# Step 5's clearing, the first batch's order, and the last batch with GEMM1's beginning

## The chip, the cores and the metric

One core of a Trainium2 chip runs the whole kernel. The metric is the device time of one execution in microseconds (us), as the median over runs.

## The reference

```python
def rmsnorm(x, g): return x / sqrt(mean(x*x, -1) + 1e-6) * g
q, k, v: (8 batches, 12 heads, 448 tokens, 64)          # float32
scores = (1/sqrt(64)) * rmsnorm(q, g_q) @ rmsnorm(k, g_k).T
attn   = exp(scores - max) / (sum + 1e-9)
x      = (attn @ v) as (3584 tokens, 768)
expert = token_ids * 2654435761 % 8                      # each token has one of 8 experts
out[mask_e] = relu(x[mask_e] @ w1[e]) @ w2[e]            # w1 (8, 768, 1024), w2 (8, 1024, 768)
```

## The kernel before

**Attention.** The work is cut into 48 steps: step s is a pair of heads of batch s // 6. For a step, `score` (L630) makes four blocks of scores in PSUM: j = 0, 1, 2 are two heads by 128 keys by 448 queries (two matmuls), j = 3 is the last 64 keys of both heads. `expo` (L647) turns each block into probabilities on ScalarE: 896 columns for j < 3, 448 for j = 3. `av_part` (L657) multiplies them with v in three parts; `row_sums` and `put_x` (L690, L697) divide by the row sums on VectorE and, after the sixth step of a batch, store the batch to `x_scratch` in HBM.

Ahead of that, q and k of a group of steps are squared (`sqq`, `sqk`, L361), summed by matmuls with an identity (`sumq`, `sumk`, L381), reduced (`redq`, `redk`), put through ln and exp on ScalarE (`ln`, `er`), multiplied in (`nq`, `nk`, L417), turned by TensorE (`Tq`, `Tk`, L588) and copied out of PSUM as `qT` and `kT` (L608; kT is scaled by a column `g_col` there). Step 0 alone is group 0, steps 1 and 2 are group 1, steps 3 to 5 are group 2. Step 5 is loaded by itself: `zero:3` (L743) clears the padding of its two raw tiles by two ScalarE copies (L756, L757), issues its six transfers on SP's queue (`load_one`, L732) and then the transfer of the token ids. All other q, k and v loads go through POOL's queue, in the order of L768 to L785.

**Who sets the order.** Each engine runs its instructions in program order, and program order is written out by hand: `emit` (L852) reads a text of tokens, `kind:step.part`, and issues each token's instructions. `@A` puts a square or a copy on ScalarE in place of VectorE, `@S` takes a PSUM tile from the ring of score tiles (3 tiles of two banks) in place of the one bank `qkT_ps`. One text covers batches 0 and 1, the text `steady` is used for each of batches 2 to 7. `spin:n` issues n dummy matmuls of 448 columns that fill TensorE's time at the start.

**The seam.** Tokens are grouped by expert. Three tiles of 128 tokens of expert 0, all from batches 0 to 6, are gathered from `x_scratch` by POOL (L230) while batch 7 runs. After the last token of `steady`, `early_xT` (L642) turns them one after the other: six transposes into a PSUM tile of the score ring (L242) and one copy into `xT_e` (L243; VectorE for tiles 0 and 1, ScalarE for tile 2). Then the last step's `av_part`, `row_sums` and `put_x` follow, and then the GEMMs.

**GEMMs.** For each expert GEMM1 (`gemm1`, L951) makes eight blocks of hidden units, each of six matmuls over 384 token columns (expert 0) or 480, with a ReLU copy each; GEMM2 (`gemm2`, L966) follows, and POOL scatters the rows of the result. Weights of later experts are loaded meanwhile. For expert 0 the routing table of the other experts is made on VectorE between the blocks.

The order around the seam, from `steady` with batch 7 as its batch: `... sc:5.0 kT:6 exp:4.1 exp:4.3 sc:5.1 rec:3 exp:5.0 sc:5.2 Tq:6 x:3 v:3 av:4.0 av:4.1 qT:6 sc:5.3 sumq:2.1 exp:5.1 exp:5.2 sqk:2.0 sc:6.0 nk:8 exp:5.3 av:4.2 ...` (tokens of steps beyond 47 issue nothing).

Of the kernel before, what the change touches and what calls it, by code (L numbers as in the profile page):

```python
# [20 lines left out]
def kernel(  # L21
# [242 lines left out]
    with tc.manual_schedule(), \  # L264
# [587 lines left out]
        def emit(text, b):  # L852
# [24 lines left out]
            sumq:2.0 redk:2.0 av:0.0 redq:2.0 sc:1.2 av:0.1 v:1 sc:1.3 ln:2 er:2 av:0.2  # L877
            sc:1.1 nq:3 rec:0 exp:1.2 exp:1.3 Tq@S:3 exp:1.1 nk:3 sc:2.0 Tk:3 x:0 exp:2.0
            sc:2.1 exp:2.1 qT:3 kT:3 sc:2.2 av:1.0 exp:2.2 sc:2.3 av:1.1 av:1.2 sqk:3.0
            sc:4.0 exp:2.3 nk:5 sumk:3.0 rec:1 exp:4.0 sc:3.0 x:1 sc:3.1 av:2.0 redk:3.0  # L880
            av:2.1 sqk:4.0 exp:3.0 nq:5 sumk:4.0 v:2 sc:3.2 av:2.2 redk:4.0 sqq:3.0 rec:2
            exp:3.1 Tk@S:5 sc:3.3 kT:5 x:2 sumq:3.0 exp:3.2 sc:4.3 sc:4.2 exp:3.3 redq:3.0
            exp:4.3 ln:3 er:3 sc:4.1 exp:4.2 av:3.0 sqk:4.1 Tq:5 exp:4.1 sqq:4.0 av:3.1 qT:5
            sumk@S:4.1 nq:6 av:3.2 nk:6 redk:4.1 sc:5.0 rec:3 sumq:4.0 sc:5.3 sc:5.1 exp:5.0
            exp:5.3 redq:4.0 sqq:4.1 x:3 Tk:6 exp:5.1 Tq@S:6 kT:6 sumq@S:4.1 redq:4.1 qT@A:6
            av:4.0 av:4.1 ln:4 sc:5.2 av:4.2 er:4 exp:5.2 sc:6.0 sqk:5.0 v:4 sc:7.0 sumk:5.0
            exp:6.0 rec:4 sc:6.3 x:4 av:5.0 av:5.1 exp:7.0 exp:6.3 nq:8 sc:7.3 redk:5.0 nk:8
            exp:7.3 v:3 Tq:8 sc:6.1 av:5.2 qT:8 sc:6.2 Tk@S:8 rec:5 sqq:5.0 exp:6.1 sc:7.1
            sumq:5.0 x:5 exp:6.2 av:6.0 sc:7.2 exp:7.1 exp:7.2 kT:8 sc:8.0 sqq:5.1 redq:5.0
            sc:8.1 nq:10 exp:8.0 av:6.1 sumq:5.1 nk:10 redq:5.1 exp:8.1 av:6.2 sc:8.3 rec:6  # L890
            Tk:10 x:6 sc:9.0 sc:8.2 exp:8.3 av:7.0 sc:9.3 exp:9.0 kT:10 Tq:10 av:7.1 av:7.2
            sc:9.1 sqk:5.1 qT:10 exp:8.2 rec:7 sc:9.2 x:7 v:5 exp:9.3 exp:9.1 sumk:5.1
            redk:5.1 exp:9.2 sqq:6.0 av:8.0 av:8.1 av:8.2 sc:10.0 sc:10.2 sc:10.1 rec:8 ln:5
            er:5 x:8 nk:12 exp:10.0 sumq:6.0 av:9.0 exp:10.1 sc:10.3 redq:6.0 Tk:12 av:9.1
            nq:12 av:9.2 kT:12 rec:9 exp:10.2 sc:11.0 exp:10.3 exp:11.0 sc:11.2 exp:11.2
            sc:11.3 x:9 Tq:12 sqq:6.1 av:10.0 av:10.1 sc:11.1 qT:12 nk:14 av:10.2 exp:11.3
            sc:12.0 sumq:6.1 sc:12.2 rec:10 exp:11.1 sc:12.1 x:10 exp:12.0 exp:12.2 redq:6.1
            Tk:14 sc:12.3 sqk:6.0 exp:12.1
# [25 lines left out]
    with tc.manual_schedule(), \  # L924
# [26 lines left out]
        def gemm1(w1v, xT, h_sb, c0, c1, both=True, after=()):  # L951
            for fo in range(FO):
                h_ps = ps_h.tile([P, 512], FP32, name="h_ps")
                for co in range(CO):
                    nc.tensor.matmul(h_ps[:, :c1 - c0], lhsT=w1v[:, co, fo, :],  # L955
                                     rhs=xT[:, co, c0:c1],
                                     start=(co == 0), stop=(co == CO - 1))
# [320 lines left out]
```

## Time and profile before

| | |
|---|---|
| Median of 3 runs | 338.56 us (337.82 to 338.94) |
| The profiled execution | 337.33 us |
| Its span | 335.8 us |
| TensorE (PE) busy | 322.8 us, 96% |
| VectorE (DVE) busy | 197.7 us, 59% |
| ScalarE (ACT) busy | 188.2 us, 56% |
| GpSimd (POOL) busy | 147.0 us, 44% |

Times of rows are microseconds from the span's start. A timeline row has the start, the length, engine, line, operation, the tiles written and read with their shapes, how many instructions are merged in it (x), and in brackets the idle time before it with what ended it. Lengths of neighbours overlap, since an instruction's end includes its write; what an engine needs for one in a dense row is the distance of starts. A row of windows has, for each stretch, its length, each engine's busy time with its count of instructions, the granted TensorE clock (1.00 is 2.4 GHz), the DMA engines' share and GB/s. A row of DMA issues has the tiles, the issuing queue, count, KB each, and us from issue to landing.

### The profile page before, as it was taken

To read this page: it belongs to the slowest core of one execution; us is meant where nothing else is said; L and a number is where in the kernel's file an instruction comes from. 1 tells how busy PE (TensorE), PEld (TensorE's weight loads), DVE (VectorE), ACT (ScalarE), POOL (GpSimd) and SP (SyncE) were. 2 spreads that over 40 slices of the span, in tenths; PEclk is the share of its full clock that TensorE was granted. 3 is DMA by queue.
4 is the path that set the end of the run, shared out by engine and by line. 5 is a ranking of instruction groups with operands and counts; after the bars stand their busy time and mean duration, and the time that the engine had idled before them with its cause. 6 is when DMAs were issued, how large, how long until landed. Compare 5 with 4: busy or idle time off the path is not lost. (4 is left out here: it accounts for less than half of the span.)

```text
span 335.8 us, 9161 instructions
## 1 busy us (share of the span) xinstructions
PE 322.8 (96%) x3873; PEld 224.9 (67%) x3873; DVE 197.7 (59%) x427; ACT 188.2 (56%) x287; POOL 147.0 (44%) x207
## 2 busy tenths in 40 slices
PE   6899999999999999998999999999999999999992
PEld 3567776777777776666677667677676676766761
DVE  4699999998989899984792342232332323222210
ACT  3799999999999999998442211212022020221211
POOL 8799925423440100003655844538556374203122
PEclk9999999999999999999999999999999999999997
DMA  6999999999999999432587899999999999923012
GB/s 118 205 202 204 214 228 197 242 200 237 203 243 210 248 227 236 84 84 72 156 169 224 162 209 247 264 280 247 255 262 263 268 254 265 267 34 133 25 64 105
DMA packets 45602, 65.54 MB, mean 195 GB/s; under 512 B 12727, under 2 KB 33423, under 8 KB 45432
## 3 DMA queue, kind: packets, MB, share of 16 engines
q0 software_dynamic: 39072, 58.32, 86.0%
q1 hardware_dynamic: 6328, 6.50, 7.2%
q8 instruction: 31, 0.51, 0.6%
q10 hardware_dynamic: 160, 0.11, 0.1%
q14 instruction: 11, 0.09, 0.1%
HBM read 89.29 MB, written 17.30 MB: 317 GB/s over the span
## 5 line engine op out<-in xcount | busy, mean ns | idle before, releaser
L652 ACT ACTIVATE expT<-sc_ps 128x896 bf16<-128x896 f32 x144 | 125.0, 960 | 0.9 <-PE sc_ps L636 0.6
L972 PEld LDWEIGHTS <-h_sb 128*128 128x128 f16 (+1 forms) x512 | 51.3, 104 | 30.2
L972 PE MATMUL o_ps<-w_sb,h_sb 128*128 128x512 f16 (+3 forms) x384 | 66.2, 326 | 0.0
L985 POOL DMA_INDIRECT out_dram<-o_sb,gidx x32 | 33.8, 1055 | 63.4 <-ACT o_sb L982 30.9
L959 ACT ACTIVATE h_sb<-h_ps 128x480 f16<-128x480 f32 (+1 forms) x36 | 19.9, 553 | 67.3 <-PE h_ps L955 67.3
L230 POOL DMA_INDIRECT kr<-x_scratch,gidx x32 | 32.7, 1022 | 50.8 <-DVE oc L578 36.7
L955 PEld LDWEIGHTS <-w_sb 128*128 128x128 f16 x288 | 38.9, 136 | 16.2
L955 PE MATMUL h_ps<-xT,w_sb 128*128 128x480 f16 x240 | 49.4, 366 | 0.0
L982 ACT COPY o_sb<-o_ps 128x768 f32<-128x768 f32 x16 | 12.8, 799 | 60.4 <-PE o_ps L972 55.2
L961 DVE TENSOR_SCALAR h_sb<-h_ps 128x480 f16<-128x480 f32 x28 | 18.4, 658 | 47.2 <-PE h_ps L955 47.2
L636 PE MATMUL sc_ps<-qT,kT 64*128 64x448 f16 x288 | 44.4, 356 | 0.7 <-DVE qT L628 0.4
L671 PEld LDWEIGHTS <-expT 128*128 128x128 bf16 x864 | 37.8, 97 | 9.0 <-DVE x_sb L702 4.1
L671 PE MATMUL av_ps<-v,expT 128*128 128x65 bf16 x846 | 42.3, 193 | 0.1
L982 DVE COPY o_sb<-o_ps 128x768 f32<-128x768 f32 (+1 forms) x15 | 14.3, 956 | 37.1 <-PE o_ps L972 30.3
L305 POOL DMA_DIRECT2D vr<-in_v_dram x36 | 23.7, 669 | 20.1 <-DMA kr<-in_k_dram 10.8
L702 DVE TENSOR_TENSOR x_sb<-av_ps,srec 128x448 f16<-128x448 f32 x47 | 29.2, 622 | 1.3
L655 ACT ACTIVATE expT<-sc_ps 128x448 bf16<-128x448 f32 x48 | 28.6, 599 | 0.1
L386 PEld LDWEIGHTS <-ident 128*128 128x128 f16 x576 | 22.6, 97 | 8.2 <-issue 3.6
L676 PE MATMUL av_ps<-v,expT 128*128 128x130 bf16 x141 | 24.5, 220 | 0.0
L972 PE MATMUL o_ps<-kr,h_sb 128*128 128x512 f16 (+3 forms) x128 | 21.6, 326 | 0.0
L243 DVE COPY xT<-xT_ps 128x768 f16<-128x768 f16 (+1 forms) x21 | 11.0, 524 | 17.9 <-PE xT_ps L242 17.7
L955 PE MATMUL h_ps<-xT,qr 128*128 128x480 f16 x96 | 19.8, 366 | 0.0
(218 smaller groups left out, 437.9 us busy)
## 6 DMA issues: line engine op xcount, KB each, us to landing
w_sb<-in_moe_w_dram POOLq DMA_DIRECT2D x18, 512.0 KB, 12.4
w_sb<-in_moe_w_dram POOLq DMA_DIRECT2D x8, 768.0 KB, 13.1
kr<-in_k_dram POOLq DMA_DIRECT2D x7, 672.0 KB, 14.9
qr<-in_q_dram POOLq DMA_DIRECT2D x7, 672.0 KB, 12.4
x_scratch<-x_sb SPq DMA_DIRECT2D x15, 288.0 KB, 6.8
...
```

Source lines behind the costliest of these rows:

```text
L230: nc.gpsimd.indirect_dma_start(out=xg[0:idx.shape[0], :], out_offset=None, in_=x_dram[0:rows, :], in_offset=bass.IndirectOffsetOnAxis(ap=i ...
L305: eng.dma_start(out=dst[64 * half:64 * half + 64, :, s0:s0 + cnt, :].rearrange("p n s d -> p n (s d)"), in_=runs(t, h0 + HP * hh, 1, n, to ...
L636: nc.tensor.matmul(sc[:, hh, :S], lhsT=kT[64 * hh:64 * hh + 64, P * j:P * j + P], rhs=qT[64 * hh:64 * hh + 64, :], start=True, stop=True)
L652: nc.scalar.activation(expT[:, 2 * j:2 * j + 2, :], sc[:, :, :S], AF.Exp, bias=0.0, scale=1.0)
L655: nc.scalar.activation(expT[:, 6, :], sc[:, 0, :S], AF.Exp, bias=0.0, scale=1.0)
L671: nc.tensor.matmul(av[:, 2 * t + hh, :], lhsT=expT[:, tl(hh, j), P * t:P * t + P], rhs=v8[:, i, vs(hh, j), 0:D + 1], start=(hh == 0 and t ...
L676: nc.tensor.matmul(av[:, 2 * t:2 * t + 2, :], lhsT=expT[:, 6, P * t:P * t + P], rhs=v8[:, i, 0::7, 0:D + 1], start=False, stop=False)
L702: nc.vector.tensor_tensor(out=xs[b][:, :, hp * D:hp * D + D], in0=av[:, :, :D], in1=srec[:, :, None].to_broadcast([P, SL, D]), op=ALU.mult)
L955: nc.tensor.matmul(h_ps[:, :c1 - c0], lhsT=w1v[:, co, fo, :], rhs=xT[:, co, c0:c1], start=(co == 0), stop=(co == CO - 1))
L972: nc.tensor.matmul(o_ps[d0 > 0][0:w, d0:d1], lhsT=h_sb[:, fo, col * P:col * P + w], rhs=w2_sb[:, fo, d0:d1], start=(fo == 0), stop=(fo == ...
L982: (nc.vector.tensor_copy if col % 2 else nc.scalar.copy)(o_sb[0:w], o_ps[0][0:w])
L985: scat = nc.gpsimd.indirect_dma_start(out=out[:, :], out_offset=bass.IndirectOffsetOnAxis(ap=idx[0:w], axis=0), in_=o_sb[0:w], in_offset=N ...
```

## The change

1. `zero:3` clears step 5's padding by two VectorE memsets, and stands later in the order, so that step 5's six transfers and the token ids are issued later.
2. Batches 0 and 1 get a new order. In its beginning both squares of step 0 and both of its copies out of PSUM are on ScalarE; of later copies, those of kT for steps 3, 5 and 6 are on ScalarE, and qT of step 6 and `sqq:2.0.1` (step 5's q) come to VectorE.
3. Batch 7 gets an order of its own, `tail`, in which expert 0's turns (`turn`) and the last step's products (`last`) stand among the others. The last step's products run over j first, so that only those with j = 2 need the third block of probabilities and only part 1 the fourth.
4. `xT_e` is laid out by token tile first; GEMM1 of expert 0 makes the first 256 columns of its first two blocks before their last 128 (`apart=2`).

```diff
-    xT_e = m_xe.tile([P, CO, CAP], FP16, name="xT_e")
+    xT_e = m_xe.tile([P, CAP // P, CO, P], FP16, name="xT_e")
@@ put_xT
-        (copy or nc.vector.tensor_copy)(xT[:, :, col * P:col * P + n], xT_ps[:, :, 0:n])
+        dst = xT[:, col] if xT is xT_e else xT[:, :, col * P:(col + 1) * P]
+        (copy or nc.vector.tensor_copy)(dst[:, :, 0:n], xT_ps[:, :, 0:n])
@@ early_xT and av_part take their PSUM tile by flag: S score ring, Q qkT_ps, else av_ps
+        def bank_of(flag):
...
+        def av_last(part):
...
+            if part == 0:
+                bank = bank_of(flag)
...
+                for j in range(3):
+                    for hh in range(2):
+                        for t in range(3):
+                            nc.tensor.matmul(pend[s][1][:, 2 * t + hh, :],
+                                             lhsT=expT[:, tl(hh, j), P * t:P * t + P],
...
+                return
+            for t in range(3):
+                nc.tensor.matmul(av[:, 2 * t:2 * t + 2, :], lhsT=expT[:, 6, P * t:P * t + P],
...
+            for j in range(4):
+                for hh in range(2):
+                    nc.tensor.matmul(av[64 * hh:64 * hh + 64, 6, :],
...
@@ zero
-                z = warm[:, 0:4 * D].rearrange("p (s d) -> p s d", d=D)
-                nc.scalar.copy(raw(1, HP - 1)[:, 0::7], z[:, 0:2])
-                nc.scalar.copy(raw(0, HP - 1)[64:P, 3::4], z[64:P, 0:2])
+                V.memset(raw(1, HP - 1)[:, 0::7], 0.0)
+                V.memset(raw(0, HP - 1)[64:P, 3::4], 0.0)
                 load_one(HP - 1)
                 setup1()
@@ the order of batches 0 and 1, its first lines
-            zero:0 zero:1 zero:2 zero:6 zero:7 spin:11 sqk:0.0 zero:3 sqq@A:0.0 sumk@S:0.0
-            redk:0.0 sumq@S:0.0 ln:0.1.2 redq:0.0 er:0.1.2 ln:0.0.1 er:0.0.1 sqk@A:1.0
-            gain:0 spin:2 nk:0 spin:4 gain:1 Tk@S:0 nq:0 sumk@S:1.0 gain:2 sqq:1.0 Tq@S:0
-            redk:1.0 sumq:1.0 kT:0 redq:1.0 qT@A:0 sc:0.0 ln:1 er:1 sc:0.1 spin:5 exp:0.0
-            nk:1 Tk@S:1 sc:0.3 nq:1 Tq:1 sqk:2.0.0 kT:1 qT:1 exp:0.1 sqq:2.0.0 v:0
-            sqk@A:2.0.1 sc:0.2 exp:0.3 sumk@S:2.0 sc:1.0 sqq@A:2.0.1 exp:0.2 exp:1.0
...
+            zero:0 zero:1 zero:2 zero:6 zero:7 spin:11 sqq@A:0.0 sumq@S:0.0 redq:0.0
+            sqk@A:0.0 ln:0.0.1 gain:0 er:0.0.1 sumk@S:0.0 gain:1 redk:0.0 ln:0.1.2 spin:8
+            er:0.1.2 zero:3 gain:2 nk:0 sqk@A:1.0 Tk:0 nq:0 Tq@S:0 kT@A:0 sumk@S:1.0 sqq:1.0
+            qT@A:0 redk:1.0 sumq@S:1.0 sc:0.0 redq:1.0 ln:1 sc:0.1 sc:0.2 er:1 nq:1 exp:0.0
+            nk:1 v:0 spin:3 spin:1 Tq:1 qT:1 exp:0.1 Tk@S:1 kT:1 sqk:2.0.0 sc:0.3 exp:0.2
+            exp:0.3 av:0.0 sc:1.0 sqq:2.0.0 sqk@A:2.0.1 sc:1.1 exp:1.0 sc:1.2 sumk:2.0
+            exp:1.1 sqq:2.0.1 av:0.1 sumq@S:2.0 redk:2.0 exp:1.2 av:0.2 v:1 redq:2.0 sc:2.0
+            v:2 rec:0 ln:2 er:2 nk:3 sc:2.2 x:0 sc:1.3 Tk:3 exp:2.0 nq:3 nq:5 exp:1.3 sc:2.3
+            av:1.0 exp:2.2 sqk:3.0 av:1.1 Tq@S:3 qT:3 sc:2.1 exp:2.3 kT@A:3 Tq@S:5 exp:2.1
...
@@ batch 7
+        tail = """
+            av:-1.0 av:-1.1 sc:1.0 kT:2 av:-1.2 exp:0.3 exp:1.0 nq:2 sc:1.1 nq:4 rec:-1
...
+            rec:2 x:2 sc:4.1 sc:4.3 av:3.0 av:3.1 av:3.2 rec:3 sc:5.0 exp:4.1 exp:4.3 sc:5.1
+            av@Q:4.0 x:3 av:4.1 exp:5.0 turn@S:0 sc:5.2 exp:5.1 av:4.2 rec:4 x:4 sc:5.3
+            exp:5.2 exp:5.3 turn@S:1 last:0 turn@Q:2 last:1 rec:5 x:5
+        """
         for b in range(2, B):
-            emit(steady, b)
-        for kt in range(KT - 1):
-            early_xT(kt)
-        for part in range(3):
-            av_part(NS - 1, part)
-        row_sums(NS - 1)
-        put_x(NS - 1)
+            emit(steady if b < B - 1 else tail, b)
@@ gemm1(..., apart=0), called with apart=2 for expert 0
+            for fo in range(apart):
+                products(fo, c0, c1 - P)
             for fo in range(FO):
...
+                products(fo, c1 - P if fo < apart else c0, c1)
+                h_ps = banks.pop(fo)
```

## Rows read from the trace of the kernel before

**Rows 1.** Busy time of each engine by stage, from the view of windows.

```profile
40.00:140.00 100.00, 99.17 (x1833) 72.14 (x1830) 94.16 (x208) 99.58 (x148) 26.10 (x37) 1.00 1.20 220
140.00:160.00 20.00, 18.57 (x324) 12.77 (x325) 13.58 (x35) 18.62 (x27) 3.15 (x3) 1.00 0.25 66
160.00:318.00 158.00, 158.00 (x1058) 108.62 (x1057) 56.16 (x101) 34.60 (x57) 79.13 (x87) 1.00 0.87 212
```

**Rows 2.** Timeline of TensorE at the seam.

```profile
157.44 0.93 PE L242 MATMUL sc_ps<-ident,kr 128*128 128x128 f16 x12 [0.32 <-ACT expT L652]
158.21 0.53 PE L671 MATMUL av_ps<-v,expT 128*128 128x65 bf16 x12
...
159.03 0.32 PE L685 MATMUL av_ps<-v,expT 128*64 128x65 bf16 x8
159.28 2.12 PE L955 MATMUL h_ps<-xT_e,w_sb 128*128 128x384 f16 x12
```

**Rows 3.** Timeline of ScalarE at the seam.

```profile
154.67 2.71 ACT L652 ACTIVATE expT<-sc_ps 128x896 bf16<-128x896 f32 x3
157.08 0.74 ACT L655 ACTIVATE expT<-sc_ps 128x448 bf16<-128x448 f32 x1
158.41 0.80 ACT L243 COPY xT_e<-sc_ps 128x768 f16<-128x768 f16 x1 [0.58 <-PE sc_ps L242]
```

**Rows 4.** Timeline of POOL: the third gather of expert 0's tokens.

```profile
153.99 1.00 POOL L230 DMA_INDIRECT kr<-x_scratch,gidx  x1 [0.30 <-issue]
```

**Rows 5.** DMA issues in the stretch of that gather: its time to landing.

```profile
kr<-x_scratch,gidx POOLq DMA_INDIRECT x1, 3.1
```

**Rows 6.** Timeline of VectorE at the seam: step 46's output, the first two turns.

```profile
156.92 0.62 DVE L702 TENSOR_TENSOR x_sb<-qkT_ps,srec 128x448 f16<-128x448 f32 x1
157.46 1.06 DVE L243 COPY xT_e<-sc_ps 128x768 f16<-128x768 f16 x2
```

**Rows 7.** Timeline of ScalarE over batches 0 and 1.

```profile
5.72 0.63 ACT L372 ACTIVATE sq_q<-expT 128x512 f16<-128x512 f32 x1 [2.60 <-DMA expT<-in_q_dram]
...
10.18 0.54 ACT L622 ACTIVATE qT<-sc_ps 128x448 f16<-128x448 f16 x1 [0.88 <-PE sc_ps L601]
...
11.90 1.71 ACT L652 ACTIVATE expT<-sc_ps 128x896 bf16<-128x896 f32 x2
...
16.25 0.92 ACT L652 ACTIVATE expT<-sc_ps 128x896 bf16<-128x896 f32 x1 [0.36 <-PE sc_ps L636]
...
22.66 3.40 ACT L652 ACTIVATE expT<-sc_ps 128x896 bf16<-128x896 f32 x4
...
31.13 0.94 ACT L622 ACTIVATE qT<-sc_ps 128x896 f16<-128x896 f16 x1
```

**Rows 8.** Timeline of VectorE at the start: a memset, step 0's norms, group 1's squares.

```profile
1.59 0.11 DVE L741 MEMSET expT<- 64x64 f32 x1
...
7.63 1.28 DVE L434 TENSOR_TENSOR n_one<-expT,rr 128x512 f16<-128x512 f32 x2
...
9.95 0.63 DVE L374 TENSOR_TENSOR sq_q<-qr 128x896 f16<-128x896 f16 x1 [0.97 <-DMA qr<-in_q_dram]
```

**Rows 9.** Timeline of TensorE at the start: six spins, the first scores.

```profile
7.12 1.29 PE L791 MATMUL av_ps<-hi 128*128 128x448 f16 x6
...
11.15 0.55 PE L636 MATMUL sc_ps<-qT,kT 64*128 64x448 f16 x4
```

**Rows 10.** Timeline of SP: step 5's first four issues and its last.

```profile
3.59 2.42 SPq L305 DMA_DIRECT2D kr<-in_k_dram  x4
...
6.76 0.61 SPq L299 DMA_DIRECT2D qr<-in_q_dram  x1
```

**Rows 11.** DMA issues: step 5's k and q from SP; v issued at 8.86 by POOL.

```profile
kr<-in_k_dram SPq DMA_DIRECT2D x1, 64.0 KB, 4.0
...
qr<-in_q_dram SPq DMA_DIRECT2D x1, 96.0 KB, 5.9
...
vr<-in_v_dram POOLq DMA_DIRECT2D x1, 96.0 KB, 7.8
```

More of the change, by code (lines that the diff above doesn't have):

```diff
@@ L640, in score @@
                                  start=True, stop=True)
+        def bank_of(flag):
+            if flag == "S":
+                return ps_sc.tile([P, 2, 512], FP32, name="sc_ps")[:, 0]
+            if flag == "Q":
+                return ps_qk.tile([P, 512], FP32, name="qkT_ps")
+            return ps_av.tile([P, 512], FP32, name="av_ps")
         def early_xT(kt):
-            bank = ps_sc.tile([P, 2, 512], FP32, name="sc_ps")[:, 0]
+            bank = bank_of(flag)[:]
             put_xT(xg_e[:, kt], xT_e, kt, bank.bitcast(FP16)[:, 0:DIN],
@@ L661, in av_part @@
             if part == 0:
-                bank = (ps_qk.tile([P, 512], FP32, name="qkT_ps") if s == NS - 2 else
-                        ps_av.tile([P, 512], FP32, name="av_ps"))
+                bank = bank_of(flag)
                 pend[s] += [bank[:, 0:SP].rearrange("p (a d) -> p a d", a=SL), bank]
@@ L688, in av_part @@
                                          start=False, stop=(j == 3))
+        def av_last(part):
+            s = NS - 1
+            c = chunk_of[s]
+            i, v8 = s - chunks[c], v8_tiles[c % NV8]
+            vs = lambda hh, j: (0, 7)[hh] if j == 3 else 1 + 3 * hh + j
+            tl = lambda hh, j: 6 if j == 3 else 2 * j + hh
+            expT = pend[s][0]
+            if part == 0:
+                bank = bank_of(flag)
+                pend[s] += [bank[:, 0:SP].rearrange("p (a d) -> p a d", a=SL), bank]
+                for j in range(3):
[3 more added lines that the diff above has]
+                                             lhsT=expT[:, tl(hh, j), P * t:P * t + P],
+                                             rhs=v8[:, i, vs(hh, j), 0:D + 1],
+                                             start=(j == 0 and hh == 0 and t == 0), stop=False)
+                return
+            av = pend[s][1]
+            for t in range(3):
+                nc.tensor.matmul(av[:, 2 * t:2 * t + 2, :], lhsT=expT[:, 6, P * t:P * t + P],
+                                 rhs=v8[:, i, 0::7, 0:D + 1], start=False, stop=False)
+            for j in range(4):
+                for hh in range(2):
+                    nc.tensor.matmul(av[64 * hh:64 * hh + 64, 6, :],
+                                     lhsT=expT[:, tl(hh, j), 384:448],
+                                     rhs=v8[:, i, vs(hh, j), 0:D + 1],
+                                     start=False, stop=(j == 3))
         def row_sums(s):
@@ L846, in gain @@
             g_mul(part, pend.get("g"))
-        setup_ops = {"zero": zero, "gain": gain, "spin": spin}
+        setup_ops = {"zero": zero, "gain": gain, "spin": spin, "turn": early_xT, "last": av_last}
         flag = ""
@@ L877 @@
[L877 to L898, printed above, removed]
+            zero:0 zero:1 zero:2 zero:6 zero:7 spin:11 sqq@A:0.0 sumq@S:0.0 redq:0.0
+            sqk@A:0.0 ln:0.0.1 gain:0 er:0.0.1 sumk@S:0.0 gain:1 redk:0.0 ln:0.1.2 spin:8
+            er:0.1.2 zero:3 gain:2 nk:0 sqk@A:1.0 Tk:0 nq:0 Tq@S:0 kT@A:0 sumk@S:1.0 sqq:1.0
@@ new lines @@
+            av:1.2 rec:1 qT:5 x:1 sc:4.0 sumk:3.0 exp:4.0 nk:5 sc:3.0 exp:3.0 sc:4.1 av:2.0
+            redk:3.0 av:2.1 sqk:4.0 Tk@S:5 sumk:4.0 sqq:3.0 exp:4.1 sc:3.1 redk:4.0 kT@A:5
+            exp:3.1 sqk:4.1 av:2.2 rec:2 sumq:3.0 redq:3.0 sc:3.2 exp:3.2 sumk@S:4.1 sc:3.3
+            ln:3 sqq:4.0 sumq:4.0 x:2 exp:3.3 redk:4.1 er:3 sc:4.2 redq:4.0 sc:5.0 sqq:4.1
+            sc:4.3 av:3.0 nk:6 sumq:4.1 v:3 exp:4.2 av:3.1 redq:4.1 exp:4.3 nq:6 exp:5.0
+            av:3.2 rec:3 ln:4 x:3 sc:5.3 sqk:5.0 Tk:6 exp:5.3 er:4 Tq@S:6 av:4.0 qT:6 sc:5.2
@@ new lines @@
+            kT@A:6 exp:5.2 nk:10 sc:5.1 av:4.1 av:4.2 sc:6.0 nq:8 sc:7.0 sumk:5.0 exp:5.1
+            exp:6.0 Tq@S:8 rec:4 x:4 redk:5.0 av:5.0 exp:7.0 sc:6.3 nk:8 av:5.1 exp:6.3
+            sc:7.2 qT:8 sc:7.1 sc:6.2 exp:7.2 sqq:5.0 sqk:5.1 av:5.2 rec:5 sumq:5.0 exp:7.1
+            Tk@S:8 redq:5.0 sumk:5.1 sqq:5.1 sc:6.1 redk:5.1 exp:6.2 kT:8 sc:7.3 sumq:5.1
+            x:5 exp:6.1 sc:8.0 exp:7.3 redq:5.1 nq:10 sc:8.2 av:6.0 Tk:10 exp:8.0 av:6.1
+            ln:5 av:6.2 exp:8.2 sc:9.0 sc:8.1 v:4 kT:10 er:5 sc:9.2 exp:9.0 rec:6 Tq:10 x:6
@@ new lines @@
+            av:7.0 exp:8.1 sqq:6.0 av:7.1 qT:10 exp:9.2 nq:12 sc:8.3 sc:9.1 av:7.2 rec:7
+            sumq:6.0 x:7 redq:6.0 nk:12 sc:10.0 exp:8.3 sc:10.2 exp:9.1 Tq:12 sc:9.3 sqq:6.1
+            exp:10.0 exp:10.2 av:8.0 av:8.1 qT:12 exp:9.3 av:8.2 sc:10.1 sc:11.0 exp:10.1
+            rec:8 Tk:12 x:8 sc:10.3 av:9.0 av:9.1 av:9.2 kT:12 rec:9 x:9 exp:11.0 sc:11.2
+            sc:11.1 sumq:6.1 exp:10.3 sqk:6.0 sc:11.3 av:10.0 v:5 exp:11.2 av:10.1 sc:12.0
+            exp:11.1 exp:11.3 redq:6.1 nk:14 av:10.2 sc:12.1 exp:12.0 rec:10 exp:12.1
@@ L899 @@
+            sc:12.2 x:10 Tk:14 exp:12.2 sc:12.3
         """, None)
@@ L949, in gemm1_late, with gemm1, products @@
                                      h_ps[:, 0:4 * n].rearrange("p (i t) -> p i t", i=4), AF.Relu)
-        def gemm1(w1v, xT, h_sb, c0, c1, both=True, after=()):
-            for fo in range(FO):
[L953 to L957, printed above, removed]
+        def gemm1(w1v, xT, h_sb, c0, c1, both=True, after=(), apart=0):
+            banks = {}
+            def products(fo, a0, a1):
+                if fo not in banks:
+                    banks[fo] = ps_h.tile([P, 512], FP32, name="h_ps")
+                dst = banks[fo][:, a0 - c0:a1 - c0]
+                if xT is xT_e:
+                    dst = dst.rearrange("p (k t) -> p k t", t=P)
+                for co in range(CO):
+                    src = xT[:, a0 // P:a1 // P, co, :] if xT is xT_e else xT[:, co, a0:a1]
+                    nc.tensor.matmul(dst, lhsT=w1v[:, co, fo, :], rhs=src,
+                                     start=(co == 0), stop=(co == CO - 1))
+            for fo in range(apart):
+                products(fo, c0, c1 - P)
+            for fo in range(FO):
+                products(fo, c1 - P if fo < apart else c0, c1)
+                h_ps = banks.pop(fo)
                 if fo % 2 == 0 or not both:
@@ L1204 @@
             if e == 0:
-                gemm1(w1_view(e, w1_sb), xTs[e], h_sb, 0, EARLY, False, after)
+                gemm1(w1_view(e, w1_sb), xTs[e], h_sb, 0, EARLY, False, after, 2)
             else:
```

6 lines of the change are left out of this document (5 added, 1 removed).

## The prediction

> **What bounds the kernel now.** I read the windows first. From 160 us on TensorE is busy in every microsecond of 158 [rows 1], so what comes earlier there ends earlier by as much: the GEMMs move as a block, and an edit ahead of them counts by what it does to the start of GEMM1, at 159.28 [rows 2]. From 40 to 140 us TensorE (99.17 of 100), ScalarE (99.58) and VectorE (94.16) are all nearly full [rows 1]. No one of them can be relieved alone: what a batch is ahead or behind at its start it keeps. From 140 us on TensorE and VectorE have room (18.57 and 13.58 of 20), and ScalarE's exponentials follow one another without a gap to their end at 157.82 [rows 1, 3]. So two places are open: the first 23 us, where engines wait for loads and for one another, and the 1.46 us between the last exponential's end and GEMM1. The timelines of these two places give the rest.
>
> **The seam: term -0.8.** Before, the third 896-column block of the last step ends at 154.67 + 2.71 = 157.38, and TensorE then does, in this order, twelve transposes (157.44 to 158.21, 0.77), all products of the last step (158.21 to 159.28, 1.07) and GEMM1 [rows 2, 3]. ScalarE's copy of the third turn ends at 158.41 + 0.80 = 159.21, just as late [rows 3]. In the new order turns 0 and 1 and the products with j = 0 and 1 stand where TensorE waits for exponentials. What is left after 157.38 is: a third of the eighteen narrow products, 6 x 0.031 = 0.19 (twelve take 0.53 with the last one's latency of some 0.16); one turn, half of 0.77 = 0.39; then `last:1`, three wide and eight half products, 0.15 + 0.25 = 0.40 (the eight are 159.03 to 159.28, the wide ones 0.05 each, what is left of the 1.07) [rows 2]. That is 157.44 + 0.98 = 158.42, which is 0.86 earlier. `last:1` needs the fourth block, which ends at 157.82 [rows 3]: it is there. Off this I take 0.06, because `sc:5.2` now stands behind turn 0 and comes about when ScalarE is ready for it.
>
> Four things must be ready by then. The third gather, issued at 153.99, lands 3.1 later, at 157.1 [rows 4, 5], and its turn starts at 157.6. The second turn's copy is behind step 46's output on VectorE, which ends at about 157.46; it takes 0.55, so it is done at 158.0 [rows 6]. The third turn's copy (0.80 on ScalarE, 158.1 to 158.9) would have held GEMM1; the 12 products of 256 columns with which `apart` begins cover it: two thirds of 12 x 0.163 = 1.3 us, to 159.7 [rows 2]. `turn@Q:2` takes over the bank of step 46, free at 157.5. The bounds are -0.3 (one of the four is late, as in the rivals) and -1.1 (the seam loses nothing and `sc:1.0`, now ahead of `av:-1.2`, closes a small gap of ScalarE at the batch's start).
>
> `apart` splits twelve matmuls in two, with twelve weight loads more: the columns are the same, 12 x 0.163 us [rows 2]; for the twelve extra starts I take +0.05 (0 to +0.2). The layout of `xT_e` makes its copies contiguous, three chunks of 128 columns for a matmul: 0, bound by 0.1 either way.
>
> **The start: term 0.** *Up to the first exponential.* Both squares of step 0 are on ScalarE now; q's begins at 5.72 when q lands and takes 0.63 [rows 7], k's follows 0.52 later, so k's sums come some 0.5 us later than when VectorE made its squares, and the norms start near 8.1, not 7.63 [rows 8]. The two memsets (0.11 each for a like shape [rows 8]) stand behind the reduction, in the time in which VectorE waits for ScalarE's ln and exp: hidden. The two ScalarE copies that go were hidden too, in its wait of 2.60 for q [rows 7]. `spin:8` costs 8 x 0.19 = 1.5 us of TensorE (six took 1.29 with latency [rows 9]) from about 7.8, so `Tk:0` starts at 9.3, though k is normed at 8.8. Copies: kT (0.54, like qT's of the same width [rows 7]) 9.8 to 10.4, qT to 10.9; first scores 10.95 against 11.15 [rows 9]. What goes is VectorE's wait of 0.97 for group 1's q, behind which kT stood [rows 8]: step 5's transfers no longer precede it, and kT no longer stands behind it. ln and exp of group 1 precede the first exponential as before: 11.75 against 11.90 [rows 7].
>
> *Up to the end of step 2.* ScalarE now does the four exponentials of step 0 in a row, and only one of step 5's squares (0.63) before step 1, which begins at 15.1 to 15.5 instead of 16.25 [rows 7]. The other square is VectorE's, at 15.4, and needs step 5's q. SP issued the six transfers from 3.59, the last at 6.76 [rows 10]; now they wait for the memsets, at 7.75, which puts the last at 10.9. Such transfers took 4.0 to 5.9 us [rows 11]: landing between 14.9 and 16.8. Followed engine by engine, with q there at 15.4 the exponentials of step 2 end and step 4's begin at 22.3, against 22.66 [rows 7]: -0.36; with q at 16.8, VectorE stands 1.4 us with group 2's reduction, a copy of v, step 0's reciprocal and step 3's norms behind it, ScalarE waits a microsecond for `ln:2`, and step 4 begins at 23.15: +0.5. I take 16.0, between: 0. The token ids move behind step 5 on SP; their first reader is in batch 5. Nothing else stands in SP's queue until batch 0 is stored.
>
> *The rest of batches 0 and 1.* ScalarE copied one qT of 896 columns (0.94 [rows 7]); now it copies kT of 512 and of 1024. From 0.54 at 448 and 0.94 at 896 these are 0.60 and 1.05 (estimate from [rows 7]); 0.15 of each overlaps its neighbour, so +0.56 for ScalarE, and some 0.5 less for VectorE. Covered as long as TensorE sets the pace; without that cover +0.56, and if VectorE was the one waited for, -0.4. I take 0, because TensorE's and ScalarE's shares are alike [rows 1].
>
> A rule speaks against these copies: the Trainium skill, ScalarE: Activation LUTs (What ACT_TABLE_LOAD costs), says that each per-partition pointer operand adds about 93 ns to an activation, and kT has one as its scale where qT had none. No row here shows a scaled copy on ScalarE. By the page +0.56 would be about +0.75; nothing else here uses that.
>
> **Sum.** -0.8 + 0.05 + 0 = -0.75 on the profiled execution: 337.33 to 336.58. The median of the runs stands 1.23 above that execution (338.56), so 337.8. The smallest change that a measurement of this kernel tells from none is about 0.3%, 1.0 us.
>
> **Rivals.** *Both places gain (0.28).* Step 5's q is in time, -0.36, ScalarE's extra is covered, and the seam gives its full -1.1: -1.4, 337.2. For it: TensorE stood idle in the first 16 us, and fewer loads now precede group 1's. Against it: the landing by the rows is later than 15.4.
>
> *ScalarE's copies count (0.12).* The seam as forecast, but ScalarE is what batches 0 and 1 wait for: -0.75 + 0.56, 338.4. For it: 99.58 of 100 [rows 1]. Against it: TensorE at 99.17 beside it.
>
> *The seam is held by something else (0.08).* The third gather lands later or the second copy waits on VectorE, and GEMM1 starts with that: -0.3, 338.3. For it: 0.5 us between landing and turn is all there is. Against it: gathers and turns are ordered by the same steps as before.
>
> *Step 5 comes too late, slower (0.14).* Its q stands in the DMA engines among the loads of group 2 and batch 1. At 7.8 us to landing, as v issued at 8.86 took [rows 11], it lands at 18.7. From the two cases above each microsecond behind 15.4 costs 0.61: -0.36 + 3.3 x 0.61 = +1.65; ScalarE starved then has no cover for its 0.56 later, and with the seam's -0.75 the sum is +1.45: 340.0. The point from which the change is slower than before is a landing at about 17.2. Against it: SP's transfers were 4.0 to 5.9 when POOL's queue had loads in it too [rows 11]. The Trainium skill, DMA: Bandwidth & Descriptors (Queues, rings and completion order), says that each DMA engine takes turns between the queues that have work, packet by packet; by that SP's few transfers don't stand behind POOL's long queue. The trace agrees in so far as SP's 5.9 lay below POOL's 7.8.
>
> **How the numbers follow.** The forecast has 0.38, its own range is 337.4 to 338.2, and a third of it lies beyond 1.0 us. Faster: 0.28 + 0.12 = 0.40. Slower: 0.14. Within: 0.46. The range goes from 336.5 (the first rival with VectorE's relief of 0.4 on top, and some scatter) to 339.4 (the late landing, but not its far end).
>
> **What would show it.** Right: GEMM1's first product 0.7 to 0.9 after the third last block's end less than before, that is about 1.0 us after it instead of 1.90; turns 0 and 1 ahead of the last exponential; `sqq:2.0.1` on VectorE with a wait below 1 us; the fourth step's first exponential within 0.5 of 22.66. Wrong: a wait of more than 1.5 us on DMA of step 5's q; ScalarE's exponentials of the last batch with gaps of more than 0.2; GEMM1 waiting on a copy of `xT_e`; batch 2 starting later than before by more than the first 23 us explain, which would be ScalarE's copies.

## The result, and the profile after

The changed kernel took 342.95 us in the median of four runs (340.51 to 344.84), the kernel before 338.75 beside it: a ratio of 1.0123, with a 95% interval of 1.0082 to 1.0163. It is slower by some 4 us, outside the predicted range. Its profiled execution took 344.55 us with a span of 342.9, against 337.33 and 335.8 before, so the traces show 7.1 us of difference: the traced execution is one of the two longest of the four.

Where it arises is quickly found. The first store of batch 1 is issued at 61.48 instead of 54.99, which is 6.5 later; from there to the first store of batch 5 it is 70.91 against 70.86, and GEMM1 starts 6.59 later. So all but 0.6 of the 7.1 us lies ahead of that store; 0.5 more comes behind the start of GEMM1. The store in the kernel before, then in the changed one:

```profile
54.99 0.45 SPq L716 DMA_DIRECT2D x_scratch<-x_sb  x1
```

```profile
61.48 0.45 SPq L752 DMA_DIRECT2D x_scratch<-x_sb  x1
```

Timeline of ScalarE in the changed kernel:

```profile
11.43 2.52 ACT L660 ACTIVATE expT<-sc_ps 128x896 bf16<-128x896 f32 x3
13.83 0.56 ACT L663 ACTIVATE expT<-sc_ps 128x448 bf16<-128x448 f32 x1
16.79 0.63 ACT L373 ACTIVATE sq_k<-kr 128x512 f16<-128x512 f32 x1 [2.40 <-DMA kr<-in_k_dram]
17.32 2.52 ACT L660 ACTIVATE expT<-sc_ps 128x896 bf16<-128x896 f32 x3
21.26 0.24 ACT L406 ACTIVATE ss<-ss 128x44 f32<-128x44 f32 x1 [1.42 <-DVE ss L402]
...
28.95 2.60 ACT L660 ACTIVATE expT<-sc_ps 128x896 bf16<-128x896 f32 x3 [0.48 <-PE sc_ps L637]
```

The first exponential is earlier than before (11.43, [rows 7] had 11.90). Then ScalarE, whose queue has step 5's k squares ahead of step 1's exponentials, waits 2.40 us for that k. Step 4's first exponential is the row at 28.95; it was 22.66 [rows 7]. VectorE waits for step 5's q, and TensorE behind both:

```profile
18.84 0.69 DVE L375 TENSOR_TENSOR sq_q<-qr 128x512 f16<-128x512 f32 x1 [2.32 <-DMA qr<-in_q_dram]
```

```profile
17.47 0.79 PE L387 MATMUL qkT_ps<-sq_k,ident 128*128 128x88 f16 x16 [2.19 <-ACT sq_k L373]
19.59 1.35 PE L387 MATMUL sc_ps<-sq_q,ident 128*128 128x88 f16 x16 [0.88 <-DVE sq_q L375]
23.56 1.04 PE L595 MATMUL qkT_ps<-ident,n_k 128*128 128x128 f16 x8 [0.92 <-DVE n_k L435]
```

The same sixteen matmuls of 88 columns take 0.79 at 17.47 and 1.35 at 19.59. The windows say why: TensorE had work for 1.66 of the 4 us from 14 to 18, and from 19 to 28 the granted clock (seventh number behind the stretch, before DMA share and GB/s) is 0.50, that is 1.2 GHz in place of 2.4.

```profile
14.00:18.00 4.00, 1.66 (x27) 1.10 (x28) 1.63 (x3) 1.60 (x3) 2.43 (x4) 1.00 1.30 215
18.00:19.00 1.00, 0.70 (x19) 0.55 (x15) 0.16 (x1) 1.00 (x3) 0.77 (x2) 0.82 1.29 203
19.00:28.00 9.00, 7.50 (x74) 5.13 (x74) 6.80 (x12) 5.55 (x10) 8.21 (x23) 0.50 1.36 201
28.00:29.00 1.00, 1.00 (x17) 0.55 (x17) 0.54 (x3) 0.52 (x2) 1.00 (x3) 0.56 1.25 198
```

SP's issues and their landings, against [rows 10, 11]:

```profile
7.66 2.47 SPq L306 DMA_DIRECT2D kr<-in_k_dram  x4
10.17 1.22 SPq L299 DMA_DIRECT2D qr<-in_q_dram  x1
11.44 1.29 SPq L300 DMA_DIRECT2D qr<-in_q_dram  x1
```

```profile
kr<-in_k_dram SPq DMA_DIRECT2D x2, 64.0 KB, 5.8
qr<-in_q_dram SPq DMA_DIRECT2D x1, 96.0 KB, 7.3
```

The last q was issued at 11.44 and landed 7.3 later, at 18.74; before it took 5.9.

At the seam the new order does about what was forecast: GEMM1 starts 1.15 us after the end of the last step's third block (162.18 + 2.54 = 164.72), instead of 1.90; the forecast was about 1.0.

```profile
162.18 2.54 ACT L660 ACTIVATE expT<-sc_ps 128x896 bf16<-128x896 f32 x3 [0.77 <-PE sc_ps L637]
```

```profile
162.35 0.50 PE L242 MATMUL sc_ps<-ident,kr 128*128 128x128 f16 x6
...
164.15 0.50 PE L242 MATMUL sc_ps<-ident,kr 128*128 128x128 f16 x6
164.48 0.70 PE L710 MATMUL av_ps<-v,expT 128*128 128x65 bf16 x18
165.02 0.50 PE L242 MATMUL qkT_ps<-ident,kr 128*128 128x128 f16 x6
165.36 0.34 PE L717 MATMUL av_ps<-v,expT 128*128 128x130 bf16 x3
165.62 0.32 PE L721 MATMUL av_ps<-v,expT 128*64 128x65 bf16 x8
165.87 2.15 PE L1001 MATMUL h_ps<-xT_e,w_sb 128*128 128x256 f16 x24
```

But ScalarE has a gap of 0.77 ahead of step 5's exponentials, which [rows 3] doesn't have; whether the new order makes it is a question for the experiments.

### The profile page after: what moved, and what is told of

The parts are those of the page before. It is cut to its first block, busy times and chain, and to the rows that moved or that the text cites. A ratio compares the mean times of both kernels' runs of the same rounds, so it can differ in the third digit from the quotient of the medians.

```text
span 342.9 us, 9188 instructions
## 1 busy us (share of the span) xinstructions
PE 327.5 (96%) x3886; PEld 228.7 (67%) x3886; DVE 198.5 (58%) x426; ACT 189.9 (55%) x288; POOL 148.0 (43%) x207
## 5 line engine op out<-in xcount | busy, mean ns | idle before, releaser
L1036 POOL DMA_INDIRECT out_dram<-o_sb,gidx x32 | 35.0, 1093 | 61.6 <-ACT o_sb L1033 29.6
L1001 PEld LDWEIGHTS <-w_sb 128*128 128x128 f16 x300 | 39.7, 135 | 16.0 <-issue 0.3
```

The lines of the kernel that those rows point to most:

```text
L1001: nc.tensor.matmul(dst, lhsT=w1v[:, co, fo, :], rhs=src, start=(co == 0), stop=(co == CO - 1))
L1036: scat = nc.gpsimd.indirect_dma_start(out=out[:, :], out_offset=bass.IndirectOffsetOnAxis(ap=idx[0:w], axis=0), in_=o_sb[0:w], in_offset=N ...
```

## The experiments

The theory: step 5's loads, issued late, stall ScalarE and VectorE, TensorE runs dry, its clock falls, and that is the whole loss. The rivals: the new order of the first batch costs by itself; the last batch has a part; the stall does it without the clock. This table collects what the traces of all kernels show: the first store of batch 1 (start and first two batches), the way from batch 5's first store to GEMM1 (the seam) with ScalarE's gap ahead of step 5's exponentials in it, and from GEMM1 to the end of the span. From batch 1's store to batch 5's, every one took 70.86 to 70.94.

| Kernel | Store of batch 1 | To GEMM1 (gap) | GEMM1 to end | Time, ratio to before (95%) |
|---|---|---|---|---|
| before | 54.99 | 33.43 (0) | 176.52 | |
| before again | 55.25 | 33.46 (0) | 176.62 | |
| changed | 61.48 | 33.48 (0.77) | 177.03 | 1.0123 (1.0082 to 1.0163) |
| e1_early | 56.34 | 33.66 (0.93) | 177.17 | 0.9997 (0.9984 to 1.0011) |
| e2_late | 60.20 | 34.39 (0.86) | 177.14 | 1.016 (1.0128 to 1.0192) |
| e3_seam | 55.43 | 33.93 (1.21) | 177.16 | 0.9975 (0.9957 to 0.9993) |
| e4_spins | 59.49 | 33.56 (0.85) | 177.11 | 1.0079 (1.0035 to 1.0123) |
| e5_first | 55.90 | 34.26 (0.71) | 176.92 | 1.0018 (1.0 to 1.0035) |
| e6_klate | 55.52 | 33.72 (1.00) | 176.94 | 1.0012 (0.9991 to 1.0034) |
| e7_qlate | 55.55 | 34.00 (1.28) | 177.02 | 0.9998 (0.9969 to 1.0028) |
| e9_tail | 55.16 | 33.54 (0.73) | 176.83 | 0.9988 (0.997 to 1.0006) |
| e10_qonly | 58.00 | 32.75 (0) | 176.98 | 1.0057 (1.0034 to 1.0081) |
| e11_konly | 59.27 | 32.63 (0) | 176.91 | 1.0053 (1.0026 to 1.008) |
| e12_spins2 | 57.02 | 32.62 (0) | 176.95 | 1.0044 (1.0019 to 1.0069) |

**The loads alone, taken away.**

```diff
-            zero:0 zero:1 zero:2 zero:6 zero:7 spin:11 sqq@A:0.0 sumq@S:0.0 redq:0.0
+            zero:0 zero:1 zero:2 zero:3 zero:6 zero:7 spin:11 sqq@A:0.0 sumq@S:0.0 redq:0.0
-            er:0.1.2 zero:3 gain:2 nk:0 ...
+            er:0.1.2 gain:2 nk:0 ...
```

> The changed kernel with one edit: step 5 is cleared (by VectorE still) and its loads are issued at the place where the kernel before did it, ahead of the group of step 0, not after the reduction of its squares. Theory (late landing): k and q of step 5 land before their squares are due, ScalarE's wait of 2.40 us and VectorE's of 2.32 us for them go, TensorE keeps the granted clock at 1.00 from 18 to 29 us, step 4's first exponential comes at 22.2 to 22.9 us instead of 28.95, and the median falls to 337.6 to 338.6. Rival (the new order of the first batch costs by itself, with two squares of step 0 and two kT copies on ScalarE): step 4's first exponential stays behind 24 us and the median stays above 340.

339.27 us, beside 339.39 for the kernel before on the same chip. By its ratio the loss is gone, though the median is above the figure expected, as is that of the kernel before. The squares of step 5's k follow the exponentials without a wait:

```profile
15.70 0.56 ACT L663 ACTIVATE expT<-sc_ps 128x448 bf16<-128x448 f32 x1
16.12 0.65 ACT L373 ACTIVATE sq_k<-kr 128x512 f16<-128x512 f32 x1
16.64 2.55 ACT L660 ACTIVATE expT<-sc_ps 128x896 bf16<-128x896 f32 x3
```

Step 4's first exponential is at about 23.8 (the second of four from 22.97), 0.9 later than expected: in this execution the clock was low earlier, 0.57 from 8 to 12, and the first exponential came at 13.31. No late load precedes that fall; TensorE had been idle for 1.13 us ahead of it.

```profile
6.49 0.55 PE L387 MATMUL sc_ps<-sq_q,ident 128*128 128x32 f16 x16 [1.13 <-ACT sq_q L373]
```

```profile
8.00:12.00 4.00, 4.00 (x32) 2.31 (x31) 2.02 (x4) 1.92 (x5) 3.33 (x6) 0.57 1.30 214
```

**The loads alone, added to the kernel before.**

```diff
-                nc.scalar.copy(raw(1, HP - 1)[:, 0::7], z[:, 0:2])
-                nc.scalar.copy(raw(0, HP - 1)[64:P, 3::4], z[64:P, 0:2])
+                V.memset(raw(1, HP - 1)[:, 0::7], 0.0)
+                V.memset(raw(0, HP - 1)[64:P, 3::4], 0.0)
-            zero:0 zero:1 zero:2 zero:6 zero:7 spin:11 sqk:0.0 zero:3 sqq@A:0.0 ... redq:0.0 er:0.1.2
+            zero:0 zero:1 zero:2 zero:6 zero:7 spin:11 sqk:0.0 sqq@A:0.0 ... redq:0.0 zero:3 er:0.1.2
```

> The kernel before with one edit: step 5 is cleared by VectorE after the reduction of step 0's q squares and its loads are issued then; its order of the first batch, its tail and the beginning of GEMM1 stay. Theory (late landing): ScalarE, which here squares both k and q of step 5 ahead of the third exponential of step 0, waits 2 us or more for them, TensorE runs dry, the granted clock falls to about 0.5 for some microseconds, and the median is 341 to 346. Rival (the loads alone are harmless, it needs the new order): 338 to 339.5, with the clock at 1.00.

344.43 us, 5.0 above. So the late loads, with the clearing on VectorE that holds them, are enough without anything else of the change. ScalarE's and TensorE's rows, and the window after the stall:

```profile
17.81 0.63 ACT L372 ACTIVATE sq_k<-kr 128x512 f16<-128x512 f32 x1 [4.42 <-DMA kr<-in_k_dram]
```

```profile
18.49 1.33 PE L386 MATMUL sc_ps<-sq_k,ident 128*128 128x88 f16 x16 [4.50 <-ACT sq_k L372]
```

```profile
16.00:18.00 2.00, 0.00 (x0) 0.00 (x0) 0.44 (x2) 0.19 (x1) 0.32 (x2) 1.00 1.28 209
18.00:20.00 2.00, 1.51 (x18) 1.23 (x17) 0.14 (x1) 2.00 (x4) 1.86 (x3) 0.52 1.28 207
```

**The seam alone.** The first batch's order and part 3 of `zero` as in the kernel before, all else as changed.

```diff
-            zero:0 zero:1 zero:2 zero:6 zero:7 spin:11 sqq@A:0.0 ...
+            zero:0 zero:1 zero:2 zero:6 zero:7 spin:11 sqk:0.0 zero:3 sqq@A:0.0 ...
```

> The changed kernel with the first batch's order, and the place and way of clearing and loading step 5, of the kernel before: only the last batch, its turns and the beginning of GEMM1 are new. By the prediction's step for the seam: 0.75 below the kernel before, 337.5 to 338.1. By the changed kernel's trace (0.75 gained behind the third last block, 0.77 lost to a gap of ScalarE earlier in the same batch, 0.5 more in the GEMMs): 338.5 to 339.2. Rival (the tail has a part in the loss): above 340.

338.37 us: 0.85 below on the ratio, with an interval from 0.2 to 1.5. The rival falls; the prediction's 0.75 lies in the interval, and no gain at all just outside it. The new last batch by itself doesn't lose, so it is not where the loss comes from.

**TensorE kept busy during the stall.** First with 12 and 5 extra matmuls, then with 9 and 2.

```diff
+            if gi == 2:
+                for _ in range(12 if a else 5):
+                    nc.tensor.matmul(T[:, 0:448], lhsT=warm[:, 0:P], rhs=warm[:, 0:448],
+                                     start=True, stop=True)
```

> The changed kernel with 17 more matmuls of 448 columns on TensorE, whose results nobody reads: 12 between the weights of the k sums of group 2 and its k sums, 5 ahead of its q sums, so that TensorE has work while step 5's k and q are on their way. The late loads stay. Theory in its narrow form (the stall costs some 2 to 2.5 us, the low clock that follows the other 4): the granted clock stays at 1.00 from 18 to 29 us, step 4's first exponential comes at 24.5 to 26 us, the median is 340.3 to 341.5 and the runs lie closer together than 4 us. Rival (the stall alone does it, the clock is only its mark): step 4's first exponential at 28 us or later and 342 to 345.

342.09 us, inconclusive: the clock stayed at 1.00 from 16 to 30, but the extra matmuls ran until 19.35 and 21.38 and delayed the sums themselves, and the clock had been low earlier (0.59 from 8 to 12).

```diff
-                for _ in range(12 if a else 5):
+                for _ in range(9 if a else 2):
```

> As the run with 12 and 5 more matmuls on TensorE, with 9 and 2, so that they end when the squares of step 5's k and q come and delay nothing. If the granted clock stays at 1.00 from 16 to 30 us: step 4's first exponential 2 to 3.5 us later than in the kernels with early loads (23.2 to 23.8), at 25.5 to 27, and a median of 340.5 to 342, which would put the stall at some 3 us and the rest of the changed kernel's loss at the clock. Rival (the stall is all): 28 or later.

339.04 us beside 337.88, a ratio of 1.0044. ScalarE and VectorE still wait, 1.98 and 1.81 us; the clock stays; step 4's first exponential is the second of the four from 23.89, at about 24.7, and the rival falls. Both this and the median are below what was expected (25.5 to 27, and 340.5 to 342): the stall is smaller than the 3 us that the expectation gave it.

```profile
16.75 0.63 ACT L373 ACTIVATE sq_k<-kr 128x512 f16<-128x512 f32 x1 [1.98 <-DMA kr<-in_k_dram]
...
23.89 3.37 ACT L664 ACTIVATE expT<-sc_ps 128x896 bf16<-128x896 f32 x4
```

```profile
18.00:20.00 2.00, 2.00 (x46) 1.67 (x45) 1.53 (x5) 1.80 (x4) 2.00 (x4) 1.00 1.27 204
20.00:24.00 4.00, 3.44 (x56) 2.29 (x52) 3.93 (x8) 3.97 (x8) 3.74 (x8) 1.00 1.29 204
```

So of the ratio's 1.2%, some 0.4% are the stall and most of the rest is the clock: 1.5 us and 2.7. These are middle values; the interval of this run alone allows 0.6 to 2.3 us for the stall, and its medians differ by 1.2. In the traces batch 1's store is 1.4 later than in the three with early loads and a full clock (57.02 against 55.52 to 55.90) with the clock held, and 5.8 later without. Step 5's q was there 0.94 earlier in this execution (17.90 against 18.84), so up to that much of the 4.5 between them is not the clock's.

**The new first order alone**, with early loads and the old last batch: `e1_early` with `emit(steady, b)` for every batch and the old turns behind the loop.

> Only the new order of the first batch, with step 5 cleared by VectorE and loaded early as in the kernel before; the last batch and its turns run in the old order (the layout of xT_e and the split beginning of GEMM1 stay). By the prediction's term for the start (0, with ScalarE's copies hidden) it equals the kernel before. By the trace of the changed kernel with early loads, where the way from step 4's first exponential to the last batch is 0.25 us longer, it is 0.2 to 0.9 above the kernel before, and above the kernel that has the new seam alone. Rival (the new order gains once the loads are early): 0.4 or more below.

339.33 us beside 338.60: 0.6 above, as the trace had it. Some of that is the beginning of GEMM1, which is still split here (below). Its trace also shows VectorE waiting 0.76 us for batch 1's k, which the other traces with early loads don't have; step 4's first exponential comes at about 22.75 (the second of four from 21.91), and the way from there to batch 1's store is 33.15 instead of 32.3.

```profile
31.83 0.86 DVE L375 TENSOR_TENSOR sq_k<-kr 128x1344 f16<-128x1344 f16 x1 [0.76 <-DMA kr<-in_k_dram]
```

**k late, q early; and q late, k early.** `zero` is divided in two parts, one at the early place and one at the changed kernel's.

```diff
...
+            elif part == 4:
+                V.memset(raw(0, HP - 1)[64:P, 3::4], 0.0)
+                load_one_q([nc.sync] * 2, raw(0, HP - 1), HP - 1)
...
-            zero:0 zero:1 zero:2 zero:6 ...
+            zero:0 zero:1 zero:2 zero:4 zero:6 ...
```

> The changed kernel, but step 5's q is cleared and loaded early (ahead of the group of step 0); only its k stays at the late place. If k's landing is enough (theory: ScalarE waits 2.4 us for it, TensorE runs dry, the clock falls), the median stays 2 us or more above the kernel before, with a wait of ScalarE of 2 us or more ahead of step 5's k squares. If q alone did it (the only one that the prediction priced), the median falls to 338.5 to 339.8.

338.82 us, no loss. But this doesn't clear k, which was not late enough. With q's two transfers away k was there at 15.56, and the early q held up group 1, so that the first exponential came at 12.29 instead of 11.43:

```profile
15.56 0.63 ACT L373 ACTIVATE sq_k<-kr 128x512 f16<-128x512 f32 x1 [0.33 <-DMA kr<-in_k_dram]
```

> The changed kernel, but step 5's k is cleared and loaded early; only its q, two transfers, stays at the late place. With k's four issues no longer ahead of it, q is issued from 7.8 us, 2.5 us earlier than in the changed kernel, and lands at 14 to 16 us by the rows of the kernel before: VectorE's wait for it is under 0.6 us, ScalarE's for k is gone, and the median is 338.5 to 339.8. Rival (whatever is issued that late lands at 18 us or later): q's squares wait over 2 us and the median is above 340.5.

338.76 us, no loss, but the issue at 7.8 was a miss: q's transfers write no element that the memset clears, so nothing held them, and SP issued them at 6.05 and 6.76, before the memset:

```profile
6.05 0.66 SPq L299 DMA_DIRECT2D qr<-in_q_dram  x1
6.76 0.62 SPq L300 DMA_DIRECT2D qr<-in_q_dram  x1
```

```profile
7.58 0.17 DVE L791 MEMSET qr<- 64x128 f32 x1
```

In the changed kernel, then, only k waits for its memset, and q stands behind k in SP's queue. So both were tried again, later. For q a further slot is cleared, which its transfers do write:

```diff
...
+                V.memset(raw(0, HP - 1)[:, 0:1], 0.0)
...
-            er:0.1.2 zero:3 gain:2 ... sqq:1.0
+            er:0.1.2 gain:2 ... sqq:1.0 zero:3
```

> The changed kernel, but step 5's k is cleared and loaded early, and its q alone is late: q is cleared (with one more slot of 64 columns, so that both of its transfers have to wait) behind the squares of group 1's q, at about 10.9 us, so it lands at 17.5 to 19, as late as in the changed kernel. By the prediction's price (0.61 us for each microsecond behind 15.4, no clock): 1.3 to 2 above the kernel before, 340 to 340.8, VectorE waiting 1 to 2.5 us. If the clock falls too: 341.5 or more. Rival (q's lateness is covered): within 0.6 of the kernel before.

339.79 us beside 337.88, a ratio of 1.0057: 1.9 us (1.1 to 2.7), with q there at 17.58. That is the loss expected without the clock, yet the clock fell as well, for less long than in the changed kernel:

```profile
17.58 0.69 DVE L375 TENSOR_TENSOR sq_q<-qr 128x512 f16<-128x512 f32 x1 [1.97 <-DMA qr<-in_q_dram]
```

```profile
20.00:24.00 4.00, 3.35 (x38) 2.98 (x37) 2.96 (x7) 3.59 (x6) 3.64 (x10) 0.57 1.35 200
```

And k alone, with `zero:3` behind `nq:0`:

> The changed kernel, but step 5's q is loaded early, and its k alone is late: it is cleared behind the norms of step 0, at about 9.3 us, and lands at about 17, as late as in the changed kernel or a little later. Theory (a late k is enough, since ScalarE squares it ahead of step 1's exponentials): ScalarE waits 1.5 to 2.5 us, TensorE runs dry, and the median is 1.5 to 5 above the kernel before, the upper part with a lower clock. Rival (it needs both): within 0.6 of the kernel before.

339.36 us, a ratio of 1.0053: 1.8 us (0.9 to 2.7). ScalarE waits 2.63 us, TensorE 2.63 behind it, and the clock is at half:

```profile
17.25 0.63 ACT L373 ACTIVATE sq_k<-kr 128x512 f16<-128x512 f32 x1 [2.63 <-DMA kr<-in_k_dram]
```

```profile
18.00:20.00 2.00, 2.00 (x30) 2.00 (x30) 0.70 (x2) 2.00 (x3) 1.91 (x4) 0.50 1.26 204
```

By the ratios either one late costs 1.8 to 1.9 us, stall and clock together; the changed kernel has both, for 4.2. The landings are not quite its own: k came 0.46 later here than there (17.25, 16.79), the late q of the run before 1.26 earlier (17.58, 18.84).

**The gap in the last batch.** The seam alone, with the old order of the last batch up to step 4's first products.

```diff
-            av:-1.0 av:-1.1 sc:1.0 kT:2 av:-1.2 exp:0.3 exp:1.0 ...
+            exp:0.3 av:-1.0 av:-1.1 nq:2 av:-1.2 kT:2 sc:1.0 exp:1.0 ...
```

> The kernel with the new seam alone, but its last batch keeps the old order up to step 4's first products; from there the turns and products run as in the changed kernel. If the gap of 0.8 to 1.2 us of ScalarE ahead of step 5's exponentials in the last batch comes from the new order of that batch's earlier part, it is gone, and the median is 0.3 to 0.9 below the kernel with the new seam. If it comes with the turns and step 4's products themselves, nothing changes: within 0.3 of it.

338.40 us, a ratio of 0.9988, no better than the seam alone; the gap is there (0.73).

> The kernel before once more, for its trace. The execution profiled at first had no gap of ScalarE ahead of step 5's exponentials in the last batch; two kernels with the same last batch had one of 0.7 to 0.9 us. If the gap belongs to the old order too, it is there again in this execution, and the way from the store of batch 5 to GEMM1 is 34.2 to 34.4 us instead of 33.43; if the first execution is the rule, 33.4 to 33.6.

337.73 us, and a way of 33.46 with no gap: as in the first execution. But `e2_late` and `e5_first`, whose last batch has the old order, have one of 0.86 and 0.71, and `e10_qonly`, `e11_konly` and `e12_spins2`, with the changed kernel's last batch, have none. So both orders occur with the gap and without, the order doesn't decide it, and like has to be compared with like. That it goes with the execution is likely but not shown: no kernel has a trace of each kind. Without it the old order takes 33.43 and 33.46, the new 32.75, 32.63 and 32.62: 0.78 less. With it the old order takes 34.39 and 34.26, the new six times 33.48 to 34.00, on average 33.73: 0.6 less. Taken off, the gap explains the scatter: each of the six leaves 32.71 to 32.73, the two of the old order 33.53 and 33.55, which is 0.8 between them once more.

The traces without the gap also show what `apart` costs. TensorE and ScalarE at the beginning of GEMM1, in `b_before` and then in `e12_spins2`:

```profile
159.58 2.12 PE L955 MATMUL h_ps<-xT_e,w_sb 128*128 128x384 f16 x12
160.81 0.49 ACT L959 ACTIVATE h_sb<-h_ps 128x384 f16<-128x384 f32 x1 [1.30 <-PE h_ps L955]
```

```profile
160.55 2.15 PE L1005 MATMUL h_ps<-xT_e,w_sb 128*128 128x256 f16 x24
162.45 0.49 ACT L1014 ACTIVATE h_sb<-h_ps 128x384 f16<-128x384 f32 x1 [1.42 <-PE h_ps L1005]
163.00 2.11 PE L1005 MATMUL h_ps<-xT_e,w_sb 128*128 128x384 f16 x12 [0.18 <-ACT h_sb L1014]
```

The 24 halves take as long as the 12 whole ones. But the first Relu starts 1.90 after GEMM1 instead of 1.23, since two blocks are finished only at the end; TensorE then waits for a PSUM bank. Every Relu from the third on is 0.36 later after GEMM1's start (8.69 against 8.33 for the eighth), and the span from GEMM1 to the end is longer by 0.3 to 0.5 (176.91 to 176.98 against 176.52 and 176.62). In the traces with the gap this doesn't show at the end: the last Relus come late in seven of those nine, with either beginning (the eighth at up to 10.00 with the new one, and at 10.02 in `e2_late`, which has the old), and `e2_late`'s 177.14 lies among the 176.83 to 177.17 of the others.

## Why the prediction was wrong

**The start, term 0: this step failed.** It followed step 5's q alone. The k squares on ScalarE were counted with their 0.63, not with the landing of their data, though they stand ahead of step 1's exponentials, due at 14.39 here, and k came at 16.79. `e11_konly` shows that a late k alone, there at 17.25, costs 1.8 us. For q the forecast took landing at 16.0, between 4.0 and 5.9 us behind a last issue that starts at 10.9. That issue started at 11.44, because the one ahead of it took 1.22 instead of 0.66, and the landing took 7.3: 18.74. The row of before that came nearest was v's 7.8 on POOL's queue [rows 11], which the prediction used only for a rival.

**The rival "step 5 comes too late" was the right mechanism, at 0.14 and at too low a price.** Its landing, 18.7, was met to the tenth by luck: the issue was 0.5 later than it took, the transfer 0.5 shorter. Its sum was 340.0; measured were 342.95. What it lacked was k, and TensorE's clock: its 0.61 per microsecond was worked out from rows in which every matmul runs at 2.4 GHz. Held at that clock (`e12_spins2`) the loss is 1.5 us, which is the size of the rival's +1.45, though not the same sum: k's stall is in the one, ScalarE's 0.56 and a landing of q 0.8 later in the other. The rest, by the same run, is for the most part the clock. Two of the changed kernel's runs, 344.55 and 344.84, have a mean granted clock of 0.980 and 0.984, the other two, 341.35 and 340.51, of 0.993 and 0.991.

The Trainium skill, DMA: Bandwidth & Descriptors (Queues, rings and completion order), was drawn on against this rival, by its rule that an engine takes turns between queues. The trace shows that this doesn't keep a landing time: the same 96 KB took 7.3 instead of 5.9 when issued 5 us later, with two loads of 672 KB issued by POOL just then (at 11.47 and 12.31).

**The seam, term -0.8: right.** 0.78 where neither execution has the gap; turns 0 and 1 stand ahead of the last exponential, the products with j = 0 and 1 begin before the third block ends, and GEMM1 doesn't wait for the copies.

**`apart`, +0.05 (0 to +0.2): mis-sized.** It is +0.36 within GEMM1, and not from the extra starts of matmuls but from the first two Relus, which come 0.67 later.

**ScalarE's copies, term 0: right, with the copies miscounted.** From step 4's first exponential to batch 1's store the old order takes 32.33 (three times) and 32.34, the new with early loads and a full clock 32.28 and 32.38 (`e6_klate`, `e7_qlate`; the 33.15 of `e5_first` has VectorE's wait for k in it). But the +0.56 that the prediction had covered counts two copies of kT; the order has three, for steps 3, 5 and 6, so by its own figures it should have been 0.90 more, in the rival on these copies too. What was covered is more than it thought. In the changed kernel the copies took 0.69 and 1.11 to 1.15, against 0.60 and 1.05 estimated. The Trainium skill, ScalarE: Activation LUTs (What ACT_TABLE_LOAD costs), with its 93 ns for a pointer operand, agrees to 0.03.

**Up to the first exponential: better than forecast, and this is what the late loads buy.** It came at 11.43 instead of 11.75: group 1's q, no longer behind step 5, is there in time. With early loads and a full clock the new order's first exponential is at 12.24 to 12.67. With the loads early, the change adds up to about nothing: -0.78 for the seam, +0.36 for `apart`, +0.45 in batch 1's store (55.52 to 55.90, on average 55.66, against 55.21 for four executions of the old order), and `e1_early`, `e6_klate` and `e7_qlate` are at 0.9997 to 1.0012.

**A better version** is the seam alone, `e3_seam`, at 0.9975 (0.9957 to 0.9993). One that splits one block of GEMM1 instead of two, to save a part of the 0.36, was not tried.
